# One weight gradient's stores turned from direct copies into scatters with eight partitions skipped

## The chip, the cores and the metric

The kernel runs on one core of a Trainium2 chip. The metric is the time of one execution in device microseconds (us).

## The reference, cut to what matters

The reference is one decode step of a block with attention over a cache (32 heads, 8192 cached positions, 128 wide) beside a gated MLP, and its gradient:

```python
def _A_ref(x, k_cache, v_cache, wq, wo):      # x 1x1x640, caches 1x32x8192x128
    q = (x @ wq)...                           # wq 640x4096
    p = softmax(einsum("bhqd,bhkd->bhqk", q, k) * Dh ** -0.5)
    o = einsum("bhqk,bhkd->bhqd", p, v)
    return o... @ wo                          # wo 4096x640
...
_out, _vjp = jax.vjp(_f, A_x, A_k_cache, A_v_cache, A_wq, A_wo, B_w1, B_w3, B_w2)
return (_out, *_vjp(grad_out))
```

What matters is the traffic. Every K and V tile is read and a gradient of the same size is written; so are the weights. That is 303.58 MB through the core's 16 DMA engines, in bf16. The gradient of `wo` (4096 x 640, 5.2 MB) is the output that the change stores in another way.

## The kernel before

K and V stream through ten SBUF slots of 128 x 8192, loads and stores alike issued by SP as 2048 KB transfers. The weights go in eight groups of four heads, issued by GpSimd. When the heads of a group are done, VectorE overwrites the `wo` tile with its gradient, and one store takes it out; the `wq` store follows, and when it has landed, the loads of the group three further on can overwrite the tiles:

```python
dwo_v = out_5.rearrange("(h p) c -> p h c", p=P)      # row h*128 + p of the output
...
def fin_wo(g):
    G_ = grp[g]
    for hh in range(GH):                              # GH = 4 heads
        nc.vector.tensor_scalar(G_["wo"][:, hh, :], g_bc[:], G_["od"][:, hh, 0:1], None, ALU.mult)
    nc.gpsimd.dma_start(dwo_v[:, g * GH:(g + 1) * GH, :], G_["wo"][:])      # 128 x 4 x 640, 640 KB

def fin_wq(g, ci):
    ...
    if ci == NC - 1:
        nc.gpsimd.dma_start(dwq_v[:, :, g * GW:(g + 1) * GW], wq_g[:])
        grp.pop(g)
        if g + 3 < NG:
            load_group(g + 3, nc.gpsimd)
```

A tile for the MLP between heads keeps its small intermediates (`hcol`, `gu`, `sig` and others) each in a place of its own.

Of the kernel before, what the change touches and what calls it, by code (L numbers as in the profile page):

```python
# [9 lines left out]
BF16 = mybir.dt.bfloat16  # L10
F32 = mybir.dt.float32
ALU = mybir.AluOpType
ACTF = mybir.ActivationFunctionType
AX = mybir.AxisListType
PSUM = bass.MemoryType.PSUM

P = 128
# [4 lines left out]
def kernel(  # L22
# [22 lines left out]
    nc = tc.nc  # L45
    H = A_k_cache.shape[1]
# [3 lines left out]
    F = B_w1.shape[1]  # L50
# [3 lines left out]
    GH = 4  # L54
    NG = H // GH
    GW = GH * DH
    KVN = J * DH
    scale = float(DH) ** -0.5

    consts = ctx.enter_context(tc.tile_pool(name="consts", bufs=1))  # L60
# [20 lines left out]
    dwo_v = out_5.rearrange("(h p) c -> p h c", p=P)  # L81
# [5 lines left out]
    NB = (F + P - 1) // P  # L87
# [3 lines left out]
    NA = NC - 1  # L91
# [44 lines left out]
    mA = free_slots.pop(0)  # L136
# [25 lines left out]
    ident_f = consts.tile([P, P], F32, name="ident_f")  # L162
    make_identity(nc, ident_f[:])
    ident_bf = consts.tile([P, P], BF16, name="ident_bf")
    nc.vector.tensor_copy(ident_bf[:], ident_f[:])
    masks = consts.tile([P, 4], F32, name="masks")
    pm_one = masks[:, 0:2]
    nc.vector.memset(pm_one[:, 0:1], 1.0)
    nc.vector.memset(pm_one[:, 1:2], -1.0)
# [101 lines left out]
    def prep_cm(g, ps):  # L271
        nc.vector.tensor_tensor(grp[g]["cm"][:].rearrange("p t a h m -> p (t a h) m"),
                                ps.unsqueeze(2).to_broadcast([P, 4 * GH, 2]),
                                mask2.unsqueeze(1).to_broadcast([P, 4 * GH, 2]), ALU.mult)

    hd = {}
    NCH = J // 8
# [213 lines left out]
    def fin_wo(g):  # L491
        G_ = grp[g]
        for hh in range(GH):
            nc.vector.tensor_scalar(G_["wo"][:, hh, :], g_bc[:], G_["od"][:, hh, 0:1], None, ALU.mult)
        nc.gpsimd.dma_start(dwo_v[:, g * GH:(g + 1) * GH, :], G_["wo"][:])

    def fin_wq(g, ci):
        G_ = grp[g]
# [18 lines left out]
        return row[:, b * P:b * P + rows]  # L517

    blocks_f = [(b, min(P, F - b * P)) for b in range(NB)]
    hcol = consts.tile([P, NB], F32, name="hcol")  # L520

    def mlp():
        gu_ps = ps_s.tile([P, 2, 16], F32, name="gu_ps", tag="sA")
# [5 lines left out]
        dh_ps = ps_d.tile([P, NB, 32], F32, name="dh_ps", tag="dA")  # L529
# [10 lines left out]
        for c0 in range(0, D, CB):  # L540
# [3 lines left out]
            for i in range(CB // 32):  # L544
                nc.tensor.matmul(dh_ps[:, NBA:NB, :], lhsT=ident_bf[:], rhs=T3[:, :, 32 * i:32 * (i + 1)],
                                 start=False, stop=True, skip_group_check=True)
        gu = consts.tile([P, 2, NB], F32, name="gu")
        nc.vector.memset(gu[:], 0.0)
        nc.vector.tensor_copy(gu[:, :, 0:NFULL], gu_ps[:, :, 0:NFULL])
        if RB:  # L550
            nc.vector.tensor_copy(gu[0:RB, :, NFULL:NB], gu_ps[0:RB, :, NFULL:NB])
        gate = gu[:, 0, :]
        up = gu[:, 1, :]
        dhc = consts.tile([P, NB], F32, name="dhc")
        nc.vector.tensor_reduce(dhc[:], dh_ps[:], AX.X, ALU.add)
        sig = consts.tile([P, NB], F32, name="sig")
        nc.scalar.activation(sig[:], gate, ACTF.Tanh, scale=0.5)
        nc.vector.tensor_scalar(sig[:], sig[:], 0.5, 0.5, ALU.mult, ALU.add)
        silu = consts.tile([P, NB], F32, name="silu")
        nc.vector.tensor_tensor(silu[:], gate, sig[:], ALU.mult)  # L560
        nc.vector.tensor_tensor(hcol[:], silu[:], up, ALU.mult)
        hcol_bf = consts.tile([P, NB], BF16, name="hcol_bf")
        nc.vector.tensor_copy(hcol_bf[:], hcol[:])
        dgu = consts.tile([P, 2, NB], F32, name="dgu")
        nc.vector.tensor_tensor(dgu[:, 1, :], dhc[:], silu[:], ALU.mult)
        t1 = consts.tile([P, NB], F32, name="t1")
        nc.vector.tensor_scalar(t1[:], sig[:], -1.0, 1.0, ALU.mult, ALU.add)
        nc.vector.tensor_tensor(t1[:], t1[:], gate, ALU.mult)
        nc.vector.tensor_scalar(t1[:], t1[:], 1.0, None, ALU.add)
        nc.vector.tensor_tensor(t1[:], t1[:], sig[:], ALU.mult)  # L570
        nc.vector.tensor_tensor(dgu[:, 0, :], dhc[:], up, ALU.mult)
        nc.vector.tensor_tensor(dgu[:, 0, :], dgu[:, 0, :], t1[:], ALU.mult)
        dgu_bf = consts.tile([P, 2, NB], BF16, name="dgu_bf")
        nc.vector.tensor_copy(dgu_bf[:], dgu[:])
        for b, rows in blocks_f:
            wsrc = w2a[:, b, :] if b < NBA else w2b[:, b - NBA, :]
            for ci in range(NC):
# [57 lines left out]
    gate = consts.tile([P, 1], F32, name="gate")  # L635
# [22 lines left out]
    def side_v(h):  # L658
        g, hh = divmod(h, GH)
        if hh == 0 and g > 0:  # L660
            fin_wo(g - 1)
        elif hh == 1 and g > 0:
            fin_wq(g - 1, 2)
        elif hh == 2 and g + 1 < NG:
            prep_new(g + 1)
            prep_do(g + 1, 0)
        elif hh == 3 and g + 1 < NG:
            prep_cm(g + 1, hd[h]["m"][:, 324:324 + 4 * GH])
# [95 lines left out]
    for hh in range(GH):  # L764
        prep_do(0, hh)
    prep_sel(0, ps_0[:, 8:8 + 4 * GH])
    prep_cm(0, ps_0[:, 8:8 + 4 * GH])
    fill_qz(0)
    rows_pe(0, ps_0[:, 64:64 + 2 * DH], False)
    rows_act(0)  # L770
    for h in range(H):
        if h == MLP_AT:
            outers_a(h - 1)
            outers_b(h - 1)
            mlp()
        head(h)
        if h < 2:
            nc.gpsimd.tensor_copy(gate[:], hd[h]["rdot"][:])
            load_group(h + 1, nc.gpsimd)
    outers_a(H - 1)  # L780
    outers_b(H - 1)
    fin_od(NG - 1)
    fin_pe(NG - 1)
    fin_wo(NG - 1)
    for ci in range(NC):
        fin_wq(NG - 1, ci)
# [57 lines left out]
```

## Time and profile before

| | before |
|---|---|
| time, median of the first three runs | 732.79 us (732.66 to 733.52) |
| span of the profiled run | 730.6 us |
| packet time of all 16 DMA engines, divided by 16 | 722.0 us |
| of it, the 16,384 packets of 16 KB that carry K and V | 631.5 us, 616.7 ns each |
| of it, GpSimd's queue | 65.1 us |
| landing of the last 2048 KB store, and how far its sixteenth increment is behind its fifteenth | 729.6 us, 8.8 us |

The last rows are added up from the trace's record of every packet and every landing; such a store lands in 16 increments of a semaphore, and the last of them ends the wait: five times between 608 and 660 us SP issues its next load 0.07 us after a sixteenth increment, whose fifteenth came 5.2 to 6.2 us before. In the tail the lone engine carries 8 of the last store's 128 packets of 16 KB (from 723.38 us), and the sixteenth increment follows at 729.6. Three lines of the page beside them: all packets by size; the only DVE group that waits for `wo` weights, with its idle time before it and what ended it; and the `wo` stores, with the time from issue to landing.

```profile
DMA packets 27145, 303.58 MB, mean 416 GB/s; under 512 B 2807, under 2 KB 4153, under 8 KB 10441
...
L251 DVE SCALAR_TENSOR_TENSOR side<-wo_g,g_bc 128x640 bf16<-128x640 bf16 x32 | 26.2, 819 | 1.1 <-DMA wo_g<-in_A_wo_dram 0.8
...
out_dram<-wo_g POOLq DMA_DIRECT2D x8, 640.0 KB, 11.4
```

The reader is to keep three numbers for later: 27,145 packets; 0.8 us of waiting for `wo` weights; and that the mean engine works 722.0 of 730.6 us. The engines are full, and the last of them ends 8.8 us after the fifteenth.

### The profile page before, as it was taken

The page shows a single profiled execution, that of the slowest core. Times are in us where ns is not written, and L with a number is a line of the kernel's source. Part 1 is how long each engine was busy: PE and PEld are TensorE (multiplying, and loading weights), DVE is VectorE, ACT ScalarE, POOL GpSimd, SP SyncE. Part 2 cuts the span into 40 slices and gives each one's busy share as a digit, 9 for nine tenths or more (in the row PEclk, how much of TensorE's full clock was granted, in tenths as well). Part 3 has the DMA queues.
Part 4 walks back from the last instruction along what each step waited for, and adds up shares of the span by engine and source line. Part 5 has one row for each costly group of instructions (what it writes and reads, how often), then busy time and mean ns, then how long its engine had stood idle before and what let it go on. Part 6 is the DMA issues. An engine that isn't in the chain of part 4 may idle for free.

```text
span 730.6 us, 13869 instructions
## 1 busy us (share of the span) xinstructions
PE 606.6 (83%) x5669; PEld 423.1 (58%) x5669; DVE 459.3 (63%) x806; ACT 369.4 (51%) x719; POOL 29.9 (4%) x45
## 2 busy tenths in 40 slices
PE   3989589998899889988987887888898889978940
PEld 2657466666566656666655555566566556655620
DVE  4069646677757776776646765547756756667482
ACT  2650736656556556554655554545554536655510
POOL 0010110000100000001000000000000000000000
PEclk9996699999999999988998998979897969989765
DMA  9999999999999999999999999999999999999993
GB/s 354 400 411 420 425 421 432 415 429 425 417 416 426 429 427 421 430 428 426 425 428 426 431 423 427 429 428 428 427 424 429 429 427 428 428 434 426 425 393 155
DMA packets 27145, 303.58 MB, mean 416 GB/s; under 512 B 2807, under 2 KB 4153, under 8 KB 10441
## 3 DMA queue, kind: packets, MB, share of 16 engines
q1 hardware_dynamic: 21328, 276.39, 89.5%
q0 software_dynamic: 5728, 26.30, 8.9%
q8 instruction: 44, 0.72, 0.4%
q14 instruction: 21, 0.16, 0.1%
q10 hardware_dynamic: 24, 0.01, 0.0%
HBM read 151.34 MB, written 151.34 MB: 414 GB/s over the span
## 4 chain that ended last, share of the span: by engine, by line
PE 42%; DMA 41%; DVE 8%; ACT 6%; issue 1%; SPq 0%; ACTq 0%; DVEq 0%
DMA out_dram<-kv 22%; PE pT L305 20%; DMA kv<-in_A_k_cache_dram 11%; DMA kv<-in_A_v_cache_dram 7%; PE m L340 6%; PE X L417 5%; ACT KT L307 4%; PE sA L324 4%; DVE kv L450 3%; PE dA L324 2%; DMA wo_g<-in_A_wo_dram 2%; DVE side L251 1%; PE gu_ps L527 1%; ACT KT L330 1%; PE m L430 1%
## 5 line engine op out<-in xcount | busy, mean ns | idle before, releaser
L307 ACT COPY KT<-pT 128x512 f32<-128x512 f32 x512 | 289.5, 589 | 235.3 <-PE pT L305 200.6
L305 PE MATMUL pT<-ident_f,kv 128*128 128x128 f32 x2048 | 318.7, 296 | 40.6 <-DMA kv<-in_A_k_cache_dram 17.9
L305 PEld LDWEIGHTS pT<-ident_f,kv 128*128 128x128 f32 x2048 | 248.5, 154 | 97.0 <-PE pT L305 27.8
L450 DVE TENSOR_TENSOR kv<-qd,U 128x4096 bf16<-128x4096 bf16 x64 | 146.0, 2284 | 0.0
L450 DVE TENSOR_TENSOR kv<-qd,P 128x4096 bf16<-128x4096 bf16 x64 | 143.6, 2284 | 0.0
L340 PEld LDWEIGHTS m<-selc,KT 128*128 128x128 f32 x512 | 67.4, 205 | 45.8 <-ACT KT L330 34.1
L340 PE MATMUL m<-selc,KT 128*128 128x16 f32 x512 | 73.2, 276 | 22.7 <-ACT KT L330 22.5
L417 PE MATMUL X<-kv,Z 128*32 128x512 bf16 x1024 | 85.3, 462 | 1.8 <-DVE Z L434 1.8
L400 DVE SCALAR_TENSOR_TENSOR U<-m,P 128x64 bf16<-128x64 f32 x32 | 7.4, 233 | 104.9 <-PE m L340 104.9
L324 PE MATMUL dA<-KT,qz 128*32 128x512 bf16 x512 | 55.2, 418 | 0.2 <-ACT KT L307 0.2
L324 PE MATMUL sA<-KT,qz 128*32 128x512 bf16 x512 | 55.1, 421 | 0.0
L324 PEld LDWEIGHTS <-qz 128*32 128x32 bf16 x1024 | 26.6, 93 | 42.8 <-issue 41.6
L417 PEld LDWEIGHTS <-Z 128*32 128x32 bf16 x1024 | 28.6, 110 | 33.9 <-issue 16.6
L366 DVE TENSOR_REDUCE mrow<-m 128x1 f32<-128x64 f32 x32 | 7.1, 223 | 62.9 <-PE m L340 62.9
L360 ACT CAST qd<-pT 128x256 bf16<-128x256 f32 x32 | 11.9, 372 | 48.6 <-DVE kv L450 32.4
L500 DVE SCALAR_TENSOR_TENSOR wq_g<-wq_g,side 128x512 bf16<-128x512 bf16 x40 | 27.3, 683 | 0.0
L251 DVE SCALAR_TENSOR_TENSOR side<-wo_g,g_bc 128x640 bf16<-128x640 bf16 x32 | 26.2, 819 | 1.1 <-DMA wo_g<-in_A_wo_dram 0.8
L373 DVE TENSOR_REDUCE negM<-m 128x1 f32<-128x128 f32 x32 | 9.3, 291 | 24.5 <-PE m L370 24.5
L432 DVE SCALAR_TENSOR_TENSOR U<-m,P 128x128 bf16<-128x128 f32 x32 | 11.4, 355 | 18.0 <-PE m L430 18.0
L390 DVE RECIPROCAL rZ<-m 128x1 f32<-128x1 f32 x32 | 5.3, 167 | 24.1 <-PE m L384 24.1
L330 ACT COPY KT<-dA 128x512 f32<-128x512 f32 x32 | 19.3, 604 | 0.6 <-PE dA L324 0.6
L330 ACT COPY KT<-sA 128x512 f32<-128x512 f32 x32 | 19.3, 603 | 0.0
(154 smaller groups left out, 365.2 us busy)
## 6 DMA issues: line engine op xcount, KB each, us to landing
out_dram<-kv SPq DMA_DIRECT2D x64, 2048.0 KB, 31.1
kv<-in_A_k_cache_dram SPq DMA_DIRECT2D x32, 2048.0 KB, 25.2
kv<-in_A_v_cache_dram SPq DMA_DIRECT2D x32, 2048.0 KB, 26.3
out_dram<-wo_g POOLq DMA_DIRECT2D x8, 640.0 KB, 11.4
out_dram<-wq_g POOLq DMA_DIRECT2D x8, 640.0 KB, 12.9
wq_g<-in_A_wq_dram POOLq DMA_DIRECT2D x7, 640.0 KB, 13.2
wo_g<-in_A_wo_dram POOLq DMA_DIRECT2D x7, 640.0 KB, 19.3
kv<-in_B_w_dram SPq DMA_DIRECT2D x2, 1728.0 KB, 28.7
```

The source lines that it names most:

```text
L251: nc.vector.scalar_tensor_tensor(junk[:], G_["wo"][:, hh, :], 1.0, g_bc[:], ALU.mult, ALU.mult, accum_out=G_["do"][:, hh:hh + 1])
L305: nc.tensor.transpose(pT[:, k * P:(k + 1) * P], W3[:, 4 * c + k, :], ident_f[:])
L307: nc.scalar.copy(KT[:].rearrange("p k w -> p (k w)"), pT[:])
L324: nc.tensor.matmul(S_[kind][q:q + QW, :], lhsT=S_["qz"][:, o:o + QW], rhs=KTb[:, par, :], start=(c0 == 0), stop=(c0 == NCH - 2), skip_grou ...
L330: nc.scalar.copy(XS[:].rearrange("p k w -> p (k w)"), S_.pop(kind)[:])
L340: nc.tensor.matmul(S_["m"][:, b0:b0 + J].rearrange("p (c k t) -> p k c t", k=4, t=2)[:, k, :, :], lhsT=XS[:, k, :], rhs=selc[:].rearrange( ...
L360: nc.scalar.copy(qd[:].rearrange("p a d -> p (a d)"), hd[h].pop("ps_r"))
L373: nc.vector.tensor_reduce(S_["negM"][:], S_["m"][:, 2 * J:2 * J + P], AX.X, ALU.max, negate=True)
L417: nc.tensor.matmul(xg["X"][q:q + QW, :], lhsT=Z[:, o:o + QW], rhs=W[:, N4 * i:N4 * (i + 1)], start=(slot == 0 and i < 4), stop=(slot == NS ...
L432: nc.vector.scalar_tensor_tensor(S_["U2"][:], S_["V"][:, 0:J].unsqueeze(2).to_broadcast([P, J, 2]), S_["m"][:, OC + NS:OC + NS + 1], S_["P ...
L450: nc.vector.tensor_tensor(dst[:, lo * DH:hi * DH].rearrange("p (j a b) -> p j a b", a=DH // 2, b=2), vec.rearrange("p (a b) -> p a b", b=2 ...
L500: nc.vector.scalar_tensor_tensor(wq_g[:, ci, :], wq_g[:, ci, :], 1.0, dqb, ALU.mult, ALU.mult, accum_out=dxa[:, ci, g:g + 1])
```

## The change

Its visible intent is to unload a particular DMA engine. In groups 2 to 6 of 8, the `wo` gradient of each head is scattered by an index per partition; the index of partitions 32 to 39 is pushed out of bounds, so that the scatter drops them. Those eight rows go as two direct stores of four rows. The index table costs SBUF, so the MLP's small tiles move into the unused end of another tile.

```diff
+    R0, NR = 32, 8
+    G0, G1 = 2, NG - 1
+    sidx = consts.tile([P, (G1 - G0) * GH], mybir.dt.int32, name="sidx")
+    nc.gpsimd.iota(sidx[:], pattern=[[P, (G1 - G0) * GH]], base=G0 * GH * P, channel_multiplier=1)
+    skip = masks[:, 4:5]
+    nc.vector.tensor_reduce(skip, ident_f[:, R0:R0 + NR], AX.X, ALU.add)
+    nc.vector.scalar_tensor_tensor(sidx[:], skip.to_broadcast(...), float(2 * H * P), sidx[:],
+                                   ALU.mult, ALU.add)
 ...
-        nc.gpsimd.dma_start(dwo_v[:, g * GH:(g + 1) * GH, :], G_["wo"][:])
+        dst = dwo_v[:, g * GH:(g + 1) * GH, :]
+        if G0 <= g < G1:
+            for r0 in range(R0, R0 + NR, 4):
+                nc.gpsimd.dma_start(dst[r0:r0 + 4], G_["wo"][r0:r0 + 4])
+            for hh in range(GH):
+                i = (g - G0) * GH + hh
+                nc.gpsimd.indirect_dma_start(
+                    out=out_5, out_offset=bass.IndirectOffsetOnAxis(ap=sidx[:, i:i + 1], axis=0),
+                    in_=G_["wo"][:, hh, :], in_offset=None, bounds_check=H * P - 1, oob_is_err=False)
+        else:
+            nc.gpsimd.dma_start(dst, G_["wo"][:])
 ...
-    hcol = consts.tile([P, NB], F32, name="hcol")
+    mt_f = mA[:, NA * F:].bitcast(F32)
+    hcol = mt(NB)                 # mt() hands out columns of mt_f; so for gu, dhc, sig, silu, dgu, ... (cut)
```

More of the change, by code (lines that the diff above doesn't have):

```diff
@@ L165 @@
     nc.vector.tensor_copy(ident_bf[:], ident_f[:])
-    masks = consts.tile([P, 4], F32, name="masks")
+    masks = consts.tile([P, 8], F32, name="masks")
     pm_one = masks[:, 0:2]
@@ L274, in prep_cm @@
                                 mask2.unsqueeze(1).to_broadcast([P, 4 * GH, 2]), ALU.mult)
+    R0, NR = 32, 8
[4 more added lines that the diff above has]
+    nc.vector.tensor_reduce(skip, ident_f[:, R0:R0 + NR], AX.X, ALU.add)
+    nc.vector.scalar_tensor_tensor(sidx[:], skip.to_broadcast([P, (G1 - G0) * GH]), float(2 * H * P), sidx[:],
+                                   ALU.mult, ALU.add)
     hd = {}
@@ L519, with mt @@
     blocks_f = [(b, min(P, F - b * P)) for b in range(NB)]
-    hcol = consts.tile([P, NB], F32, name="hcol")
+    mt_f = mA[:, NA * F:].bitcast(F32)
+    mt_at = [0]
+    def mt(cols):
+        r = mt_f[:, mt_at[0]:mt_at[0] + cols]
+        mt_at[0] += cols
+        return r
+    hcol = mt(NB)
     def mlp():
@@ L546, in mlp @@
                                  start=False, stop=True, skip_group_check=True)
-        gu = consts.tile([P, 2, NB], F32, name="gu")
-        nc.vector.memset(gu[:], 0.0)
+        gu = mt(2 * NB).rearrange("p (w b) -> p w b", w=2)
+        nc.vector.memset(gu, 0.0)
         nc.vector.tensor_copy(gu[:, :, 0:NFULL], gu_ps[:, :, 0:NFULL])
@@ L553, in mlp @@
         up = gu[:, 1, :]
-        dhc = consts.tile([P, NB], F32, name="dhc")
-        nc.vector.tensor_reduce(dhc[:], dh_ps[:], AX.X, ALU.add)
-        sig = consts.tile([P, NB], F32, name="sig")
-        nc.scalar.activation(sig[:], gate, ACTF.Tanh, scale=0.5)
-        nc.vector.tensor_scalar(sig[:], sig[:], 0.5, 0.5, ALU.mult, ALU.add)
-        silu = consts.tile([P, NB], F32, name="silu")
-        nc.vector.tensor_tensor(silu[:], gate, sig[:], ALU.mult)
-        nc.vector.tensor_tensor(hcol[:], silu[:], up, ALU.mult)
@@ L562, in mlp @@
-        hcol_bf = consts.tile([P, NB], BF16, name="hcol_bf")
-        nc.vector.tensor_copy(hcol_bf[:], hcol[:])
-        dgu = consts.tile([P, 2, NB], F32, name="dgu")
-        nc.vector.tensor_tensor(dgu[:, 1, :], dhc[:], silu[:], ALU.mult)
-        t1 = consts.tile([P, NB], F32, name="t1")
-        nc.vector.tensor_scalar(t1[:], sig[:], -1.0, 1.0, ALU.mult, ALU.add)
-        nc.vector.tensor_tensor(t1[:], t1[:], gate, ALU.mult)
-        nc.vector.tensor_scalar(t1[:], t1[:], 1.0, None, ALU.add)
@@ L570, in mlp @@
-        nc.vector.tensor_tensor(t1[:], t1[:], sig[:], ALU.mult)
-        nc.vector.tensor_tensor(dgu[:, 0, :], dhc[:], up, ALU.mult)
-        nc.vector.tensor_tensor(dgu[:, 0, :], dgu[:, 0, :], t1[:], ALU.mult)
-        dgu_bf = consts.tile([P, 2, NB], BF16, name="dgu_bf")
-        nc.vector.tensor_copy(dgu_bf[:], dgu[:])
+        dhc = mt(NB)
+        nc.vector.tensor_reduce(dhc, dh_ps[:], AX.X, ALU.add)
+        sig = mt(NB)
+        nc.scalar.activation(sig, gate, ACTF.Tanh, scale=0.5)
+        nc.vector.tensor_scalar(sig, sig, 0.5, 0.5, ALU.mult, ALU.add)
@@ new lines, in mlp @@
+        silu = mt(NB)
+        nc.vector.tensor_tensor(silu, gate, sig, ALU.mult)
+        nc.vector.tensor_tensor(hcol, silu, up, ALU.mult)
+        hcol_bf = mt(NB // 2).bitcast(BF16)
+        nc.vector.tensor_copy(hcol_bf, hcol)
+        dgu = mt(2 * NB).rearrange("p (w b) -> p w b", w=2)
+        nc.vector.tensor_tensor(dgu[:, 1, :], dhc, silu, ALU.mult)
+        t1 = mt(NB)
+        nc.vector.tensor_scalar(t1, sig, -1.0, 1.0, ALU.mult, ALU.add)
+        nc.vector.tensor_tensor(t1, t1, gate, ALU.mult)
@@ L575, in mlp @@
+        nc.vector.tensor_scalar(t1, t1, 1.0, None, ALU.add)
+        nc.vector.tensor_tensor(t1, t1, sig, ALU.mult)
+        nc.vector.tensor_tensor(dgu[:, 0, :], dhc, up, ALU.mult)
+        nc.vector.tensor_tensor(dgu[:, 0, :], dgu[:, 0, :], t1, ALU.mult)
+        dgu_bf = mt(NB).bitcast(BF16).rearrange("p (w b) -> p w b", w=2)
+        nc.vector.tensor_copy(dgu_bf, dgu)
         for b, rows in blocks_f:
```

## The prediction

> **What bounds the kernel now.** I read the page first: the busy shares, the slices, the queues, the chain that ended last.
>
> ```profile
> PE 606.6 (83%) x5669; PEld 423.1 (58%) x5669; DVE 459.3 (63%) x806; ACT 369.4 (51%) x719; POOL 29.9 (4%) x45
> ...
> DMA  9999999999999999999999999999999999999993
> GB/s 354 400 411 420 425 421 432 415 429 425 417 416 426 429 427 421 430 428 426 425 428 426 431 423 427 429 428 428 427 424 429 429 427 428 428 434 426 425 393 155
> ...
> q1 hardware_dynamic: 21328, 276.39, 89.5%
> q0 software_dynamic: 5728, 26.30, 8.9%
> ```
>
> The reader is to see that the DMA engines are at 90% or more in every slice but the last, that no compute engine is, and that the bytes are mostly the K/V loads and stores on queue 1 (89.5% of the time of 16 engines); the transfers issued by GpSimd (queue 0) are 8.9%. Adding all packet times gives 98.8% of 16 engines over the 730.6 us span. So the 303.58 MB set the time, and only 1.2% of it, 8.4 us per engine, is idle anywhere. The last slice is short of bytes (155 GB/s), so I cut the end with the table by stretches. Its columns are the stretch, its length, the busy time of PE, PE load, DVE, ACT and POOL with counts, the granted clock, the DMA share and GB/s.
>
> ```profile
> 420.00:714.00 294.00, 246.21 (x2195) 168.00 (x2193) 184.01 (x299) 144.30 (x288) 8.93 (x11) 0.85 1.00 425
> 714.00:722.40 8.40, 0.93 (x3) 0.59 (x3) 2.90 (x15) 0.00 (x0) 0.86 (x1) 0.50 0.59 235
> 722.40:729.20 6.80, 0.00 (x0) 0.00 (x0) 0.00 (x0) 0.00 (x0) 0.00 (x0) 0.50 0.06 27
> ```
>
> This is the reading that matters. From 722.4 to 729.2 us no compute engine runs, and the DMA share is 0.06, which is 1/16: **one DMA engine works alone for 6.8 us** while fifteen are done. The DMA view of that stretch says what it moves:
>
> ```profile
> DMA packets 19, 0.18 MB, mean 27 GB/s; under 512 B 2, under 2 KB 2, under 8 KB 10
> ...
> q1 hardware_dynamic: 10, 0.15, 5.1%
> q0 software_dynamic: 9, 0.03, 1.2%
> ```
>
> That is the rest of the last K store (16 KB packets) and of the last GpSimd stores. The same shows earlier in the trace's records of landings: a DMA over 128 partitions ends with 16 semaphore increments[...], and I took for 60 large DMAs how far the sixteenth comes after the fifteenth. Mean by time: 0.1 us in 200 to 300 us, 1.7 in 300 to 400, 2.8 in 400 to 500, 4.1 in 500 to 600, 6.0 in 600 to 713, then 7.8, 9.3 and 8.8 us for the last three landings (the last at 729.6). Behind the median engine the last is 10.0 us in 600 to 713. One straggler falls behind steadily; every load and every slot waits for it, since the wait is for all sixteen. Its packets are of the same kinds as the others'; the records don't name engines, and its cause I leave open.
>
> [...]
>
> **The change part by part.** The order of instructions shows 50 rows on GpSimd becoming 76. In each of the groups 2 to 6, one store of 128x4x640 is replaced by two stores of 4x4x640 and four scatters with one 1280-byte row per partition; bytes are the same, 640 KB.
>
> *What it takes off an engine.* I read the change as an aim at the straggler: eight consecutive rows are one sixteenth of 128, so if the scatter deals out rows in sixteen runs of eight, exactly one engine (the fifth) gets nothing. Its share of one store is 8 x 4 x 1280 = 40,960 bytes, 10 packets of 4096. Those packets took 160 ns each in the tail (the packets of that size next to the lone engine's), so 1.6 us a group, **8.0 us in five groups**. All five are over before the last of the loads.
>
> *What it adds to the others.* Each row of a scatter is likely a packet of its own. Packets of 1280 bytes on queue 1 took 57 ns on average; by size, 1280/4096 of 160 ns is 50. So 7 ns x 120 rows x 4 x 5 groups = 17 us over 15 engines, 1.1 us each. The small stores carry eight rows of 5120 bytes (204 ns on average)[...]. [...]
>
> *What it does to GpSimd.* All scatters name the whole output, so the program makes each wait for the one before it: two small stores, then four round trips. The page's issue list has a wo store land 11.4 us after issue; at that, five steps are some 55 us. The gap it has to fit in is seen in the order of time on POOL:
>
> ```profile
> 297.37 0.76 POOL L495 DMA_DIRECT2D out_dram<-wo_g  x1 [27.98 <-DVE qz L347]
> 332.08 0.86 POOL L504 DMA_DIRECT2D out_dram<-wq_g  x1 [33.95 <-DVE wq_g L502]
> 345.36 0.88 POOL L111 DMA_DIRECT2D wq_g<-in_A_wq_dram  x1 [12.42 <-DMA out_dram<-wq_g]
> 346.24 0.77 POOL L113 DMA_DIRECT2D wo_g<-in_A_wo_dram  x1
> 379.58 0.76 POOL L495 DMA_DIRECT2D out_dram<-wo_g  x1 [32.57 <-DVE qz L347]
> ```
>
> The reader is to see 35 us from wo store to wq store, so the wq store may go some 20 us late and the loads after it with it: 346 becomes about 366, landing by 385 (19.3 us median). Those weights (group 5) are first read two heads before head 20, at about 422 us by the spacing of 82 to 85 us per four heads. **Slack of some 40 us: hidden.** The index table adds one GpSimd iota and two small DVE operations at the start (they are of 20 columns; some 0.5 us), before weights that come at 12.9 us; the MLP scratch moved into a free slot changes addresses only.
>
> *The sum.* The straggler's gain of 8.0 us counts only until the next engine is last. That one had its last landing 8.8 us before the end and now gets 1.1 to 3.1 us more: 5.7 to 7.7 us are left. The tail of compute can't hold this back: the last K load lands 5.7 us earlier on all other engines, so heads 30 and 31, which run without a DMA wait from 654.6 to 717 us in the chain, move by about as much. I choose 6.3 us if the aim is right, 732.8 - 6.3 = 726.5.
>
> **The rivals.** [...] *B: the skipped rows are closed up, so that 120 rows are dealt evenly.* The straggler then gets 7.5 rows of 8 and pays 1.1 us for small packets: 732 to 735. *C: rows of a scatter are slow, or go to few engines.* 2400 rows on one engine at 57 ns are 137 us, far over 2%; nothing in the trace shows a scatter, so I can't exclude it, but the split into eight skipped rows makes sense only for one who saw sixteen equal shares. [...] *E: GpSimd's serial waits reach the weight loads.* It would need 40 us more than I count.
>
> **Range and chances.** The aim being right has three chances in four for me: 725 to 728.5. A or B, about one in six: 731 to 735. C or E, about one in twelve, up to far over. Middle of all: **727.0 us, range 724.5 to 734.0**. Faster by over 2% means under 718.1, which is below the 720.8 at which the next engine ends: 0.01. Slower by over 2% means over 747.4 and needs C or E: 0.04. Within 2%: 0.95.
>
> **What would show it.** In the new profile: the stretch at DMA share 0.06 at the end is gone or under 2 us, and the sixteenth landing comes within 2 us of the fifteenth in 600 to 713; the span is shorter by what the tail lost. Right for the added cost: queue 0 has some 2400 packets of 1280 bytes at about 57 ns, and 800 of 4096 fewer. Right for GpSimd: DVE does not wait for the wo load. Wrong: the lone engine is still there and ends as late (A or B), or the landings show a new last engine with a growing distance (C or D), or waits for the weight loads appear in DVE and PE (E).

A: the scatter deals out rows by another map than sixteen runs of eight, the straggler keeps its share, and the time stays at 732 to 735 us. The sum: the next engine ends 8.8 us before the end and was given 1.1 to 3.1 us more, so 5.7 to 7.7 us are left of the 8.0; 6.3 chosen, 732.8 - 6.3 = 726.5 us. Of the added time 1.1 us is the estimate for the scatters above; the other 0 to 2.0 us stood for the four-row stores (ten packets of 0.2 us, if all fell to one engine). D was its upper end, a gain of 5.7 us. That each scattered row is a packet, and that rows go in sixteen runs of eight, were guesses that no trace had shown.

## The result, and the profile after

The changed kernel takes **736.91 us** (median of 6 runs, 734.83 to 737.19) against 732.79 (6 runs, 732.59 to 733.91): the ratio is 1.0045 with a 95% interval of 1.0031 to 1.0059. Ratios here and below are the mean time of one kernel's fast runs over that of the other's of the same rounds, so they are not quite the ratio of the medians quoted beside them. By the 2% limit that is "same", as predicted; but 736.9 lies outside the predicted range, and the sign is wrong. Run again later, it took 736.24 us beside 734.01, ratio 1.0034 (1.0021 to 1.0048). All outputs are right.

First the end of the execution, in the same table by stretches that the prediction used (length; busy time of PE, PE load, DVE, ACT, POOL; granted clock; DMA share; GB/s), now of the changed kernel:

```profile
714.00:722.40 8.40, 0.93 (x3) 0.58 (x3) 5.71 (x24) 0.00 (x0) 0.86 (x1) 0.50 0.83 329
722.40:729.20 6.80, 0.00 (x0) 0.00 (x0) 0.00 (x0) 0.00 (x0) 0.00 (x0) 0.50 0.09 39
729.20:733.70 4.50, 0.00 (x0) 0.00 (x0) 0.00 (x0) 0.00 (x0) 0.00 (x0) 0.50 0.04 16
```

The reader is to see that the lone engine is still there: the share is 0.09 from 722.4 us on, where 1/16 is 0.06, and work now goes on into the stretch after 729.2. The last landing comes at 732.7 us, 10.9 us after the fifteenth increment of the same store (before: 729.6 and 8.8). Nothing was taken off the engine that ends last.

Then the page of the changed kernel. The lines answer to those shown of before, with the scatter's group of instructions between them:

```profile
DMA packets 27704, 303.58 MB, mean 414 GB/s; under 512 B 3366, under 2 KB 4712, under 8 KB 11000
...
q1 hardware_dynamic: 21328, 276.39, 89.3%
q0 software_dynamic: 6288, 26.30, 8.9%
...
L510 POOL DMA_INDIRECT out_dram<-wo_g,sidx x20 | 32.7, 1633 | 134.6 <-DMA out_dram<-wo_g,sidx 100.6
...
L251 DVE SCALAR_TENSOR_TENSOR side<-wo_g,g_bc 128x640 bf16<-128x640 bf16 x32 | 26.2, 820 | 0.9 <-DMA wo_g<-in_A_wo_dram 0.5
```

Queue 0 has 6288 packets in place of 5728. By size, from the records: 400 more of 4 bytes (they carry the semaphore increments of 25 more transfers, 16 each), 160 of 16 bytes that were not there before, and exactly as many as before of 5120 bytes (1968) and of 4096 (2400). So a scatter of 1280-byte rows is not sent as 1280-byte packets: four rows share a packet of 5120 bytes, as in the direct store. GpSimd waits for its own earlier scatters for 100.6 us, and the only DVE group that needs the weights loaded afterwards waits 0.5 us for them, not more than before. That wait is for the first weights of all (at 13.0 us; before, 0.8 us at 12.9), so the later loads cost DVE no wait in either kernel.

The instructions of GpSimd in order of time (start, length, what it is, idle time before it and what ended it) show one group:

```profile
300.08 1.19 POOL L507 DMA_DIRECT2D out_dram<-wo_g  x2 [29.79 <-DVE qz L356]
308.05 2.51 POOL L510 DMA_INDIRECT out_dram<-wo_g,sidx  x1 [6.78 <-DMA out_dram<-wo_g]
318.54 1.03 POOL L510 DMA_INDIRECT out_dram<-wo_g,sidx  x1 [7.99 <-DMA out_dram<-wo_g,sidx]
325.94 2.19 POOL L510 DMA_INDIRECT out_dram<-wo_g,sidx  x1 [6.36 <-DMA out_dram<-wo_g,sidx]
335.73 0.98 POOL L510 DMA_INDIRECT out_dram<-wo_g,sidx  x1 [7.60 <-DMA out_dram<-wo_g,sidx]
336.70 0.94 POOL L523 DMA_DIRECT2D out_dram<-wq_g  x1
351.37 0.91 POOL L111 DMA_DIRECT2D wq_g<-in_A_wq_dram  x1 [13.73 <-DMA out_dram<-wq_g]
```

Each scatter waits for the one before it, as predicted; from the four-row stores to the `wq` store behind the fourth scatter it takes 36.6 us. The `wq` store starts at 336.7 us (before: 332.1), the next load at 351.4 (345.4): 6 us later, inside the slack.

| packet time of all engines / 16, us | before | change | change again |
|---|---|---|---|
| all packets | 722.0 | 724.0 | 725.5 |
| GpSimd's queue | 65.1 | 65.6 | 65.5 |
| K and V packets of 16 KB | 631.5 | 632.8 | 634.5 |
| mean of one such packet, ns | 616.7 | 617.9 | 619.7 |

So the scatters and small stores themselves cost 0.5 us an engine. Most of the rest of what the change added (1.3 of 2.0 us, and 3.0 of 3.5) is in K and V packets, of which there are as many as before, each a little longer. Each column is one execution.

### The profile page after: what moved, and what is told of

It is laid out like the page before. It is cut to its first block, busy times and chain, and to the rows that moved or that the text cites. A ratio compares the mean times of both kernels' runs of the same rounds, so it can differ in the third digit from the quotient of the medians.

```text
span 733.7 us, 13932 instructions
## 1 busy us (share of the span) xinstructions
PE 608.8 (83%) x5669; PEld 425.8 (58%) x5669; DVE 459.9 (63%) x808; ACT 369.1 (50%) x719; POOL 65.3 (9%) x71
## 3 DMA queue, kind: packets, MB, share of 16 engines
q0 software_dynamic: 6288, 26.30, 8.9%
## 4 chain that ended last, share of the span: by engine, by line
DMA 44%; PE 38%; ACT 7%; DVE 7%; issue 2%; SPq 0%; ACTq 0%; DVEq 0%
DMA kv<-in_A_k_cache_dram 18%; PE pT L314 17%; DMA out_dram<-kv 17%; DMA kv<-in_A_v_cache_dram 8%; PE m L349 5%; PE X L426 4%; ACT KT L316 4%; PE sA L333 3%; DVE kv L459 2%; PE dA L333 2%; DMA wo_g<-in_A_wo_dram 2%; ACT kv L627 1%; ACT KT L339 1%; PE gu_ps L554 1%; DVE side L251 1%
## 5 line engine op out<-in xcount | busy, mean ns | idle before, releaser
L510 POOL DMA_INDIRECT out_dram<-wo_g,sidx x20 | 32.7, 1633 | 134.6 <-DMA out_dram<-wo_g,sidx 100.6
L441 DVE SCALAR_TENSOR_TENSOR U<-m,P 128x128 bf16<-128x128 f32 x32 | 11.4, 355 | 18.6 <-PE m L439 18.6
L507 POOL DMA_DIRECT2D out_dram<-wo_g x10 | 6.0, 602 | 174.2 <-DVE qz L356 174.2
```

The source lines that it names most:

```text
L441: nc.vector.scalar_tensor_tensor(S_["U2"][:], S_["V"][:, 0:J].unsqueeze(2).to_broadcast([P, J, 2]), S_["m"][:, OC + NS:OC + NS + 1], S_["P ...
L510: nc.gpsimd.indirect_dma_start(out=out_5, out_offset=bass.IndirectOffsetOnAxis(ap=sidx[:, i:i + 1], axis=0), in_=G_["wo"][:, hh, :], in_of ...
```

## The experiments

In this table "gap" is how far the sixteenth increment of the last 2048 KB store comes after its fifteenth, and "K/V packet" the mean of a 16 KB packet, both in the profiled run. "Before" is the median of the kernel before on the same chip beside it.

| run | median us | before us | ratio (95% interval) | gap us | K/V packet ns |
|---|---|---|---|---|---|
| the change | 736.91 | 732.79 | 1.0045 (1.0031 to 1.0059) | 10.9 | 617.9 |
| the change, again | 736.24 | 734.01 | 1.0034 (1.0021 to 1.0048) | 11.4 | 619.7 |
| scatter of all rows | 735.08 | 733.68 | 1.0020 (1.0003 to 1.0037) | 11.0 | 617.4 |
| table and scratch, no scatter | 734.64 | 733.68 | 1.0019 (1.0003 to 1.0036) | 8.0 | 618.4 |
| the same, again | 735.42 | 734.01 | 1.0027 (1.0013 to 1.0041) | 8.4 | 618.9 |
| four direct stores by head | 735.80 | 734.01 | 1.0026 (1.0012 to 1.0040) | 8.7 | 618.5 |
| rows 92-95, 124-127 skipped | 735.19 | 733.68 | 1.0021 (1.0004 to 1.0038) | 9.8 | 618.6 |
| rows 28-31, 60-63 skipped | 735.03 | 733.68 | 1.0019 (0.9998 to 1.0039) | 8.4 | 618.5 |
| two scatters a head, by one bit | 733.77 (one run) | 734.01 | not timed | 7.8 | 617.4 |
| **rows 16-19, 48-51 skipped** | **729.38** | 734.22 | **0.9932** (0.9914 to 0.9949) | **0.6** | 618.5 |
| the same, scratch in its old place | 729.47 | 734.22 | 0.9936 (0.9920 to 0.9952) | 2.8 | 617.2 |
| the change, scratch in its old place | 735.50 | 734.22 | 1.0012 (0.9994 to 1.0029) | 10.1 | 618.3 |
| scratch moved alone | 734.27 | 734.22 | 0.9996 (0.9980 to 1.0012) | 12.4 | 616.7 |
| index table alone | 734.73 | 734.15 | 1.0015 (1.0000 to 1.0030) | 9.9 | 617.5 |
| the kernel before, against itself | 733.76 | 734.15 | 0.9995 (0.9982 to 1.0007) | 10.1 | 617.1 |

### Which part costs, and which rows would help?

After the first result I had one theory and two rivals. Theory: the scatter does not deal out rows in sixteen runs of eight, so rows 32 to 39 were not the last engine's. Rival: the skip did relieve the last engine, and the scatters cost more than that. Rival: the time went into the serial chain on GpSimd. The first pair takes the skip and the scatter away; the second skips, in each kernel, eight other rows in two runs of four, a choice that was my guess and that no run had shown.

**All rows scattered**, nothing skipped and no four-row stores (edits here and below are against the change, unless said):

```diff
-    nc.vector.tensor_reduce(skip, ident_f[:, R0:R0 + NR], AX.X, ALU.add)
+    nc.vector.memset(skip, 0.0)
...
-            for r0 in range(R0, R0 + NR, 4):
-                nc.gpsimd.dma_start(dst[r0:r0 + 4], G_["wo"][r0:r0 + 4])
```

> The changed kernel with nothing skipped: four scatters of all 128 rows in each of the five groups and no four-row stores. If the four-row stores put the extra work on the straggling engine (small-store theory), the time falls back to 732.5 to 734. If the loss comes with the scatters themselves, 20 more GpSimd transfers instead of 5 (scatter theory), it stays at 735.5 to 737.5. No packets of 16 bytes should be left in either case.

Measured: 735.08 us, ratio 1.0020; queue 0 has no 16-byte packets, and as many of 5120 bytes. The lone engine is as before. The time lies between the two expectations and settles neither. Skipping rows 32 to 39 shows no gain over skipping none: the ratio of the change is 0.15 to 0.25% higher, though from other chips.

**No scatter**, with the index table and the moved scratch kept:

```diff
-        if G0 <= g < G1:
+        if False:
```

> The changed kernel with its index table and the MLP scratch moved as changed, but every wo store made as before in one transfer. If the loss is in the new stores (both theories above), 732.5 to 733.5 as before. If it comes from the moved addresses or the extra start-up work (rival), 735.5 to 737.5.

Measured: 734.64 us, ratio 1.0019, though every store is again that of the kernel before. This too lies between its two expectations. The kernel was run again beside the change, and gave 1.0027 where the change gave 1.0034. So more than half of what the change lost there is not the scatter's, and with no scatter there is no serial chain on GpSimd either: that rival can't be this part of the loss.

**Rows 92 to 95 and 124 to 127 skipped**, and **rows 28 to 31 and 60 to 63**:

```diff
-    nc.vector.tensor_reduce(skip, ident_f[:, R0:R0 + NR], AX.X, ALU.add)
+    skq = consts.tile([P, 2], F32, name="skq")
+    nc.vector.tensor_reduce(skq[:, 0:1], ident_f[:, 92:96], AX.X, ALU.add)     # second kernel: 28:32
+    nc.vector.tensor_reduce(skq[:, 1:2], ident_f[:, 124:128], AX.X, ALU.add)   # second kernel: 60:64
+    nc.vector.tensor_reduce(skip, skq[:], AX.X, ALU.add)
...
-            for r0 in range(R0, R0 + NR, 4):
+            for r0 in (92, 124):                                               # second kernel: (28, 60)
```

> The changed kernel, but the scatters skip rows 92 to 95 and 124 to 127[...] and those go as two four-row stores. [...]the straggler loses 8 packets of 204 ns in each of five groups, 8.2 us, and the time is 726 to 731, with the lone tail nearly gone. If the straggler is another engine, or the rows are dealt otherwise, 735 to 738 with a lone tail of 9 us or more.

> The same with rows 28 to 31 and 60 to 63[...]. [...]726 to 731 and the tail nearly gone. Otherwise 735 to 738. [...]if both stay at 735 or more, the straggler is neither.

The gain in each (726 to 731) had the condition that the skipped rows are the whole share of the engine that ends last (the straggler); "neither" in the second means the engine of neither set of rows.

Measured: 735.19 and 735.03 us, ratios 1.0021 and 1.0019, gaps of 9.8 and 8.4 us. Neither took the gap away, and guessing rows one set after another was a poor use of runs.

### The trace made to name the rows

The records of packets don't name engines. But the packets of one engine follow each other closely, the next starting, by the records, 3 or 4 ns before the end of the one before (so all through the lone engine's tail in the kernel before, 722.4 to 729.2 us), so the last engine's packets can be followed back from the one that carries the sixteenth increment, in the stretches where that is unambiguous. What was missing is a mark that tells rows apart. I gave it one: by the records of the changed kernel, a scatter sends a packet of 5120 bytes for four rows that it keeps, and packets of 16 bytes when it drops rows, two in each of the 20 scatters with eight rows out. So each head's rows went in two scatters, the first with the rows where one bit of the partition number divided by four is 0, the second with those where it is 1, another bit for another head. The result stays right, and the sizes spell out the rows.

```diff
+    BITS = {2: (0, 1, 2, 4), 3: (0, 1, 2, 4), 4: (0, 1, 2, 3), 5: (0, 1, 2, 4), 6: (3, 2, 1, 0)}
+    sidx = consts.tile([P, 2, NI_], mybir.dt.int32, name="sidx")       # one table for bit 0, one for bit 1 (cut)
...
-                nc.gpsimd.indirect_dma_start(... ap=sidx[:, i:i + 1] ...)
+                for w in range(2):
+                    nc.gpsimd.indirect_dma_start(... ap=sidx[:, w, i:i + 1] ...)
```

> The rows of each head go as two scatters, the second with those rows whose quad number (row divided by four) has one given bit set, the first with the others; the bit differs from head to head (0, 1, 2, 4 in groups 2, 3 and 5). An engine shows 5120-byte packets for the rows that it moves and 16-byte packets for those skipped, so the straggler's own sequence of packets spells its two quads. [...]if scatters were dealt in runs of eight rows they would differ in bit 0. The result is right. Time: 735 to 740, since 40 scatters replace 20.

The scatters of group 6 in the order of time on GpSimd:

```profile
643.37 2.00 POOL L521 DMA_INDIRECT out_dram<-wo_g,sidx  x1 [6.07 <-DMA out_dram<-wo_g,sidx]
652.14 0.98 POOL L521 DMA_INDIRECT out_dram<-wo_g,sidx  x1 [6.77 <-DMA out_dram<-wo_g,sidx]
660.62 0.98 POOL L521 DMA_INDIRECT out_dram<-wo_g,sidx  x1 [7.50 <-DVE U L421]
667.77 1.42 POOL L521 DMA_INDIRECT out_dram<-wo_g,sidx  x1 [6.18 <-DMA out_dram<-wo_g,sidx]
675.82 1.96 POOL L521 DMA_INDIRECT out_dram<-wo_g,sidx  x1 [6.63 <-DMA out_dram<-wo_g,sidx]
683.92 1.25 POOL L521 DMA_INDIRECT out_dram<-wo_g,sidx  x1 [6.14 <-DMA out_dram<-wo_g,sidx]
691.70 0.98 POOL L521 DMA_INDIRECT out_dram<-wo_g,sidx  x1 [6.53 <-DMA out_dram<-wo_g,sidx]
700.13 2.16 POOL L521 DMA_INDIRECT out_dram<-wo_g,sidx  x1 [7.45 <-DMA out_dram<-wo_g,sidx]
```

and the packets of the last engine some 5 us after each of them, by the records:

| scatter issued at | rows that it keeps | sizes at the last engine (start, us) | reading |
|---|---|---|---|
| 643.37 | bit 3 is 0 | 5120 (648.85), 16 (649.65) | half of its rows |
| 652.14 | bit 3 is 1 | 16 (656.43), 5120 (657.08) | the other half |
| 660.62 | bit 2 is 0 | 16 (664.80) | bit 2 is 1 |
| 667.77 | bit 2 is 1 | 5120 (672.72), 5120 (673.52) | |
| 675.82 | bit 1 is 0 | 5120 (681.41), 5120 (682.21) | bit 1 is 0 |
| 683.92 | bit 1 is 1 | 16 (689.30) | |
| 691.70 | bit 0 is 0 | 5120 (697.01), 5120 (697.85) | bit 0 is 0 |
| 700.13 | bit 0 is 1 | 16 (706.16), 16 (706.79) | |
| group 5: 628.30 | bit 4 is 0 | 5120 (632.98), 5120 (633.80) | bit 4 is 0 |
| group 5: 635.41 | bit 4 is 1 | 16 (639.63), 16 (640.25) | |

The one run took 733.77 us, under the 735 to 740 expected. From the top bit down the reading is 0?100 in binary: 4 and 12, that is **rows 16 to 19 and 48 to 51**, and not the run of eight that the change leaves out.

The same following of packets in the changed kernel finds two packets of 5120 bytes at the last engine in a scatter (651.75 and 652.56 us, 669.41 and 670.26), so its share was whole. Of the two four-row stores just before, it had a packet of 16 bytes for one (642.23) and a row of 5120 bytes for the other (643.47).

### The residue, once more

**Four direct stores by head** in place of the scatters, and the change and the kernel without a scatter again:

```diff
-                nc.gpsimd.indirect_dma_start(...)
+                nc.gpsimd.dma_start(dst[:, hh, :], G_["wo"][:, hh, :])
```

> The changed kernel, but each wo store of the five groups is made as four direct GpSimd stores, one a head, with no index and no skipped row, so 20 stores where the kernel before has 5. If the cost is in the number of GpSimd transfers, 735 to 737. If it is in the scatter, 732.5 to 734.5, as with no scatter.

> The changed kernel itself, to have it beside the two others on the same chip: 735 to 737 by every theory.

> The changed kernel with every wo store direct, as in an earlier run. There it was 0.19% over the kernel before, of which its trace lost 1.6 us at once between 128 and 148 us, in the MLP stage, which the change doesn't touch in its work. If that step comes by chance, the ratio is now within 0.1% of 1; if it belongs to the moved scratch, 1.001 to 1.003 again.

Measured: ratios 1.0026, 1.0034, 1.0027. Direct stores with no index cost as much as scatters of all rows did, and with no store changed at all the loss is as large too, so by-head stores are not needed for it, though the time met the expectation for "the number of GpSimd transfers". The scatter as such is cleared of the larger part.

### The right rows, and the scratch

**Rows 16 to 19 and 48 to 51 skipped** is the edit of the two skips above with 16 and 48.

> The change with other rows skipped: 16 to 19 and 48 to 51, the rows that the packets of the identification run gave to the engine that ends last[...]. Theory (that engine is slow by itself and has these rows): it loses 8 packets of 5120 bytes at 204 ns in each of five groups, 8.2 us, the engine behind it becomes last, some 5 to 8 us earlier; the lone tail at the end is under 2 us; 728 to 731 us, ratio 0.993 to 0.997. Rival 1 (no engine is slow by itself: whichever is behind is kept behind): another engine takes its place, lone tail of 6 us or more, 734 to 737 us, as the change. Rival 2 (the packets were decoded wrongly): the engine behind still has two packets of 5120 bytes in each scatter, 734 to 737 us.

Measured: **729.38 us against 734.22, ratio 0.9932**. The table by stretches of this kernel, to its end at 728.3 us:

```profile
714.00:722.40 8.40, 0.86 (x3) 0.48 (x3) 1.12 (x5) 0.00 (x0) 0.00 (x0) 0.50 0.67 277
722.40:726.70 4.30, 0.00 (x0) 0.00 (x0) 0.00 (x0) 0.00 (x0) 0.00 (x0) 0.50 0.13 52
726.70:728.30 1.60, 0.00 (x0) 0.00 (x0) 0.00 (x0) 0.00 (x0) 0.00 (x0) 0.50 0.00 0
```

and the landings of the last wait behind the one before, in 600 to 713 us: 6.0 us in the kernel before, 7.2 in the change, 0.6 here. The transfers of this kernel are those of the change in number and size:

```profile
DMA packets 27705, 303.58 MB, mean 417 GB/s; under 512 B 3367, under 2 KB 4713, under 8 KB 11001
```

So which rows are skipped makes the difference; the edit also builds the mask in three small operations in place of one, but so do the two skips above, which gained nothing. The cleanest size is from the next pair, on one chip: the right rows and rows 32 to 39, both with the old scratch, 729.47 against 735.50 us, 0.8%. The rival that any engine which is behind is kept behind falls: no other engine took its place. The rival that the packets were decoded wrongly falls too. The rows were named on chip 12 and relieved on chip 15, so on these two the engine that ends last has the same rows; on chip 7 they were not named.

**The same, and the change, with the scratch in its old place** (another small tile at the end gives the room), and **the scratch moved alone** in the kernel before (of the first two kernels only the line that makes room is shown, against the kernel before):

```diff
-    fin_bf = consts.tile([2 * NC, P], BF16, name="fin_bf")
+    fin_bf = t_tile()[0:2 * NC, 0:P]
```

> Rows 16 to 19 and 48 to 51 skipped, and the MLP scratch left where it was before (room is made by another small tile at the end). If both theories hold (that engine is slow by itself; the moved scratch costs 0.2%): the fastest of all, 726.5 to 730 us, ratio 0.991 to 0.996, 1 to 2 us below the same skip with the scratch moved. If the scratch costs nothing: as the skip with the scratch moved. If no engine is slow by itself: 733 to 736 us.

> The change as it is (rows 32 to 39 skipped), but the MLP scratch left where it was. If the scratch costs half of the change's loss: 734 to 735 us, ratio 1.001 to 1.003. If the scatters cost all of it: 735 to 737 us, ratio 1.003 to 1.005, as the change.

> The kernel before with only the scratch of the MLP moved into the free slot; no index table, no scatter. If the moved scratch (or the place of the buffers after it) is what the kernels without any scatter lost: ratio 1.002 to 1.003, 734.5 to 736 us. If that loss came from the index table or was chance: within 0.1% of before.

Measured: 729.47 us (0.9936), 735.50 (1.0012) and 734.27 (0.9996). No cost of the scratch is seen: alone it gives the time of before (0.9980 to 1.0012), and the skip of the right rows is as fast with it as without. My expectation that undoing it gains 1 to 2 us was wrong. The change with the old scratch came out 1 us lower than the change itself, but its interval spans both that and no difference.

### What is left of the loss

Left in every slower kernel is the index table. The last two runs build **the table alone**, never used, in the kernel before, and set **the kernel before against itself**, to see what two copies of one kernel show.

> The kernel before with only the index table built at the start and never used; scratch in its old place, every store direct. If the table costs what the kernels without a scatter lost: ratio 1.002 to 1.003, 735.5 to 736.5 us. If that loss needed table and scratch together, or was chance of the runs: within 0.1% of before.

> The kernel before, run as if it were a changed one. If the ratios of 1.002 in the other runs are real effects: within 0.1% of 1. If such ratios come out of two copies of one kernel too: 1.001 or more, or 0.999 or less, and then nothing may be concluded from 0.2%.

Measured: 1.0015 (1.0000 to 1.0030) and 0.9995 (0.9982 to 1.0007). Two copies agree within 0.1% in this one comparison, and most intervals above exclude 1, so 0.2 to 0.3% in the others is probably real; but the table alone lies between the two expectations and settles neither. Inconclusive; what the profiles show is where packet time grew, in single executions on different chips. The packet time per engine of the table alone is 723.2 us against 722.0 and 722.4 in the two profiles of before, 0.8 to 1.2 us more, of which 0.4 to 0.8 us is in the K and V packets. Without a scatter, but with table and scratch, it is 724.1 and 724.2. Why those packets get longer, by some 0.4 to 2.2 ns each, I have not found.

## Why the prediction was right or wrong

**What bounds the kernel: right.** One DMA engine ends the execution and falls behind steadily (its landings 0.1 us behind the fifteenth in 200 to 300 us, 6.0 in 600 to 713, in the profile of before), and relieving it shortens the kernel. The run with the right rows shows it, 0.9932. No other engine took its place: the gap was 0.6 and 2.8 us in the two kernels that relieve it, 7.8 to 12.4 in all the others.

**The step that failed: "eight consecutive rows are one sixteenth of 128, so if the scatter deals out rows in sixteen runs of eight, exactly one engine (the fifth) gets nothing."** The runs showed a different map: four rows go in one packet of 5120 bytes, and the last engine has 16 to 19 and 48 to 51. With rows 32 to 39 skipped its share of each scatter that was followed stayed whole, two packets of 5120 bytes, so the 8.0 us of relief did not go to it, and it still landed 10.9 us after the fifteenth (before: 8.8). This was rival A, which the prediction gave with rival B "about one in six". The runs of eight were the author's assumption: no trace had shown how a scatter deals out rows. I put that story first because the choice of eight rows seemed to make sense only for an author "who saw sixteen equal shares". An author's aim, read out of a change, was taken for a fact of the chip, and under A the change could gain nothing.

**Packet sizes: wrong, of no consequence.** (So is a slip in the sum of idle time: 730.6 less 722.0 is 8.6 us, not 8.4.) I took a scatter's row for a packet of 1280 bytes and the `wo` store's packets for 4096. Both kinds of store send 5120-byte packets (4096 are those of `wq`). The scatters and four-row stores cost 0.5 us an engine in GpSimd's queue, where I had 1.1, plus 0.6 to 2.0. The 8.0 us of relief survive all the same: two packets a scatter, four scatters, five groups, at about 200 ns (the median of the 1968) are also 8.0 us (an estimate). What dropped rows cost is little: the 160 packets of 16 bytes took a mean of 11 ns each. Two come with each of the 20 scatters, 40 in all, and 24 with the two four-row stores of each group, 120 in all.

**The sum for a right aim: its size was off.** I had a gain of 6.3 us, from a floor at the next engine. With the right rows the gain was 5.0 us (0.9932 of 734). The term that was mis-sized is "1.1 to 3.1 us more" for the next engine, which is to absorb the rest: the prediction had its last landing 8.8 us before the end, at 720.8, and in the run with the right rows the second last comes at 726.0, 5.2 us later. Half a microsecond of that is the moved share (8.0 us over 15 engines), and 1.8 us is the longer packet time of the mean engine (723.8 us against 722.0). The other 2.9 us I can't place: the engines other than the last don't end together, and the fifteenth of one trace need not be the fifteenth of the other.

**GpSimd's chain: right in kind, too long in size.** The chain to the `wq` store took 36.6 us where I counted some 55, since a scatter lands a median 8.1 us after issue and a four-row store 6.3, not 11.4. The next loads came 6 us later where I had 20, and DVE waits for `wo` weights only at the start, in both kernels. Rival E was rightly put low.

**What the range missed.** For rival A the prediction had 732 to 735 us: a gain of nothing and a cost of nothing. The cost was 2 to 4 us. The sum had no term for an effect on transfers that the change doesn't touch, and there most of the added packet time lies: K and V packets 1.2 to 3.0 ns longer in the two profiles of the change, which at 1024 packets an engine are 1.3 to 3.0 us. How much of it is the table's, and by what mechanism, stays open. Open too is why that one engine is slow, but not how. In the profile of before its packets can be followed both ways from the 4-byte packets of its late sixteenth increments (those that start 470 to 525 ns before a sixteenth landing more than 2 us behind the fifteenth), as long as only one packet can be next. The 232 K and V packets found in this way between 200 and 712 us took a mean 629.4 ns, all others 614.5; in the change 387 of them took 628.9, the others 616.1. Some 15 ns on each of about 835 packets an engine between 160 and 712 us are some 12 us, an estimate, near the 10.0 us by which this engine ends behind the median one. So by these stretches it loses a little on packet after packet. Some of the longest packets come with the instruction queue's: in the profile of before the 44 packets of 16 KB on the instruction queue took a median 1.0 us each, against 0.61 us for most K and V packets of that size, and beside the end of 29 of them (1 to 16 ns before it) a K or V packet of over 0.9 us began, where only 89 of all 16,384 took that long.

## What to carry to other kernels

When a wait for sixteen engines ends late because of one of them, find out which rows that engine has before moving any: skipping different rows in each of several transfers lets packet sizes name them, at the price of one run. The same edit on wrong rows cost 0.2 to 0.45%, on the right ones it gained 0.7%. And where a change suggests a map of rows that no run has shown, test the map first; a change tells what its author meant, not what the chip does.
